# Channel attention on one Trainium2 core: one read of 24 rows issued as two, by partitions

## The chip, the cores and the metric

The kernel runs on one core of one Trainium2 chip. The metric is the device time of one execution in microseconds (us), lower is better. The core's engines are TensorE (PE), VectorE (DVE), ScalarE (ACT), GpSimd (POOL) and SyncE (SP). Data moves between the device memory and the on-chip memory of 128 partitions through 16 DMA engines, which this document calls lanes; here SP issues all reads and ACT issues all writes.

## What is computed

The input x is a picture of 384 x 384 positions with 384 channels in bf16. Per channel a mean and a maximum over all positions are taken; both go through the same two small matrices, and the sigmoid of their sum scales each channel of x:

```python
xf = x.reshape(B, H * W, C)
gap = jnp.mean(xf, 1)
gmp = jnp.amax(xf, 1)
h_a = relu(gap @ w1)
h_m = relu(gmp @ w1)
scale = sigmoid(h_a @ w2 + h_m @ w2)
return x * scale[:, None, None, :]
```

(`relu` and `sigmoid` stand here for the reference's own few lines.) The scale needs all of x, and the product needs all of x again, so the work has two passes over 113.25 MB.

## The kernel before, in words

The 147,456 positions are 1,152 rows of 128 partitions, a row being 384 channels or 768 bytes in each partition. The **first pass** reads all of them in 53 transfers that SP issues in a loop over `steps`, at one line (L371 in the listing). A transfer of m rows puts m x 768 bytes into each of the 128 partitions. For each transfer, PE adds its rows up (`sums`, L274, and `tail_sums`, L290, for the last four transfers), and DVE takes the running maximum into `acc` (`maximum`, L340). For seven groups of 32 rows, the `packed_block`, PE and ACT also squeeze the four parts of eight rows into three (`test`, `pack`; L301, L302, L322, L328, L329), so that they stay on the chip and are not read again; the parts of group i start at row `FIRST_AT[i]` (24 rows) and `FOURTH_AT[i]` (8 rows). Groups 1 to 3 are read in one transfer of 32 rows, the others in one of 24 and one of 8 (group 0's 24 in two pieces).

When the last read of the first pass has landed and DVE has folded `acc` to one row (L346 and L423 turn it over on PE), the small products run and ACT writes the sigmoid, `scale_bc`, at L431. The **second pass** multiplies rows by `scale_bc` on DVE (`multiply`, L436), writes them out from ACT's queue, and reads back what had not stayed on the chip (L529), each new read into the place that a write has left. Packed groups are opened again between these (`unpack`, L468, L473, L487).

The order is written out by hand: the loop over `steps` fixes the order of each engine's instructions. A read waits on SP until its place is free. That is mostly told by DVE, PE or ACT, which have read the rows that stood there. There are also eight landing semaphores, used in turn, so a transfer may have to wait for the one eight places ahead of it. Whoever reads `rows` waits for the landing of the transfer that brought them.

The read that the change touches is the nineteenth of the first pass, the 24 rows of packed group 4 (`FIRST_AT[4]` is 200). It is a transfer of 128 partitions with 18,432 bytes each, 2304 KB. It is followed on SP by the 8 rows of the same group (768 KB) and by the reads of the blocks behind it.

Of the kernel before, what the change touches and what calls it, by code (L numbers as in the profile page):

```python
# [39 lines left out]
FIRST_AT = (0, 104, 40, 64, 200, 176, 152)  # L40
# [12 lines left out]

FIRST_LOAD = 4
FOLD_BEFORE = 2

BETWEEN = (
    ((21, 30), (208, 48)), ((51, 21), (0, 49), (72, 21)), ((208, 51), (0, 46), (46, 34)),
# [29 lines left out]
def kernel(  # L88
# [7 lines left out]
    nc = tc.nc  # L96
    P = nc.NUM_PARTITIONS
# [9 lines left out]
    xr = x.rearrange("b h w c -> (b h w) c")  # L107
    orr = out.rearrange("b h w c -> (b h w) c")

    def rows_of(ap, block):  # L110
        first, n = block
        return ap[first * P:(first + n) * P, :].rearrange("(p n) c -> p n c", n=n)
# [7 lines left out]
    def take(n):  # L120
        nonlocal at
        at += n
        return at - n, n
# [3 lines left out]
    packed_block = take(GP * PACKED)  # L127
# [36 lines left out]
    rows = nc.alloc_sbuf_tensor_at("rows", [P, HELD_ROWS + BODY_ROWS, C], BF16, offset=RING_BYTES).ap()  # L164
# [68 lines left out]
    for i in range(PACKED):  # L233
        if i in TOGETHER:
            lo = min(HOME_AT[i], D_AT[i % 2])
# [34 lines left out]
    def sums(rows, n, done, total):  # L270
        for k in range(0, n, MM_ROWS):
            g = min(MM_ROWS, n - k)
            for q in range(CQ):
                nc.tensor.matmul(  # L274
                    sum_ps[q * QP:q * QP + 1, 0:g * P],
                    lhsT=ones_bf[:, 0:1],
                    rhs=rows[:, k:k + g, q * P:(q + 1) * P],
                    start=(done + k == 0),
                    stop=(done + k + g == total),
                )  # L280

    def turn_sums():
        for r in range(MM_ROWS):
            nc.scalar.copy(out=s_sb[r % 2], in_=sum_ps[:, r * P:(r + 1) * P])  # L284
            nc.tensor.matmul(gsum_ps, lhsT=s_sb[r % 2], rhs=pick, start=(r == 0), stop=False)

    def tail_sums(rows, n, last):
        for k in range(n):
            for q in range(CQ):
                nc.tensor.matmul(  # L290
                    gsum_ps[:, q:q + 1], lhsT=rows[:, k, q * P:(q + 1) * P], rhs=ones_bf,
                    start=False, stop=(last and k == n - 1 and q == CQ - 1),
                )
# [12 lines left out]
    def test(i, what):  # L306

        if what == 2:
            test_one(high(part(i, 3), I8), 5 * i + 4)
            return  # L310
        n = G * C // 2
        a_b = homes[i][:, 0:2 * G, :].rearrange("p (r n) c -> p r (n c)", r=2).bitcast(I8)
        test_one(a_b[:, :, 2 * n * what + 1:2 * n * (what + 1):2], 5 * i + 2 * what)
        test_one(high(part(i, 2), I8)[:, n * what:n * (what + 1)], 5 * i + 2 * what + 1)

    def pack(i, half):
        n = G * C // 2
        span = slice(half * n, (half + 1) * n)
        for c in range(0, n, BANK):
            for r in range(4):  # L320
                for k, dt in enumerate((E4, E3)):
                    nc.tensor.matmul(  # L322
                        words[:, c:c + BANK], lhsT=weights[2 * r + k],
                        rhs=high(part(i, r), dt)[:, half * n + c:half * n + c + BANK],
                        start=(r == 0 and k == 0), stop=(r == 3 and k == 1),
                    )
        for r in (0, 1):
            nc.scalar.copy(out=high(part(i, r), U8)[:, span], in_=low(part(i, r + 2), U8)[:, span])  # L328
        nc.scalar.activation(  # L329
            out=part(i, 2).rearrange("p n c -> p (n c)").bitcast(U16)[:, span], in_=words,  # L330
            func=ACT.Copy, bias=32767.5,
        )

    def judge():
        nc.scalar.activation(out=test_copy, in_=tests[:, 0:NT], func=ACT.Copy, accum_out=test_sum)
        nc.scalar.copy(out=total, in_=test_sum)
        nc.tensor.matmul(bad_ps, lhsT=total, rhs=ones_bf, start=True, stop=True)

    def maximum(out_, in0, in1):
        nc.vector.tensor_tensor(out=out_, in0=in0, in1=in1, op=ALU.max)  # L340

    def turn_over(out_, rows):

        for r in range(LATE_ROWS):
            for q in range(CQ):
                nc.tensor.transpose(  # L346
                    out=out_[:, r, q * P:(q + 1) * P], in_=rows[:, r, q * P:(q + 1) * P], identity=ident_bf
                )
# [3 lines left out]
    def fold():  # L352

        n = folds[-1]
        h = n // 2
        maximum(acc[:, 0:h, :], acc[:, 0:h, :], acc[:, n - h:n, :])
        folds.append(n - h)

    done = turn = nth = 0
    for st in steps:  # L360
        if st[0] == "test":
            test(*st[1:])
        elif st[0] == "pack":
            pack(*st[1:])
        elif st[0] == "judge":
            judge()
        if st[0] != "load":
            continue
        _, block, rows, lo, hi = st
        m = hi - lo  # L370
        nc.sync.dma_start(out=rows, in_=rows_of(xr, block)[:, lo:hi, :])  # L371
        if nth < len(loads) - SUM_TAIL:
            sums(rows, m, done, TOT - tail_rows)
        else:
            tail_sums(rows, m, nth == len(loads) - 1)
        if nth == len(loads) - FOLD_BEFORE:
            fold()
        halves = HALVES if len(folds) == 1 else ((0, folds[-1]),)
        j = max(0, min(m, A - done))
        if j:  # L380
            nc.vector.tensor_copy(out=acc[:, done:done + j, :], in_=rows[:, 0:j, :])
        done += m
        if nth == len(loads) - SUM_TAIL - 1:
            turn_sums()
        while j < m:
            c, e = halves[turn % len(halves)]
            turn += 1
            e = min(e, c + m - j)
            maximum(acc[:, c:e, :], acc[:, c:e, :], rows[:, j:j + e - c, :])
            j += e - c  # L390
        if block == late_block:
            turn_over(late, rows)
        elif block == first_block:
            nc.vector.tensor_copy(out=kept_ps.bitcast(U32), in_=rows[:, 0:PSUM_ROWS, :].bitcast(U32))
            nc.vector.tensor_copy(out=kept_b.bitcast(U32), in_=rows[:, PSUM_ROWS:for_psum, :].bitcast(U32))
        nth += 1
# [164 lines left out]
    for turn in range(turns):  # L561
        b, buf = order.pop(0)
# [56 lines left out]
```

## Time and profile before

| what | value |
|---|---|
| time, median of 3 runs | 725.32 us (725.16 to 725.88) |
| the profiled execution, its own time | 725.41 us |
| its span, first to last instruction | 723.6 us |
| bytes read / written | 192.14 MB / 113.25 MB |
| DMA packets | 20403 |
| DVE busy | 564.1 us (78% of the span) |
| ACT busy | 349.8 us (48%) |
| PE busy | 184.7 us (26%) |

The profile is that of one execution. Its page divides the span into 40 equal slices of 18.09 us and gives, for each, the busy share of each engine and of the DMA lanes and the bytes moved per second. Other views give who waited for whom, the chain of work that ended last, the instructions in order of time, and busy time by stretch. For every transfer the trace also keeps sixteen landing marks, one for each lane that has finished its share, and a record of every packet with its start, length and size.

### The profile page before, as it was taken

The page shows a single profiled execution, that of the slowest core. Times are in us where ns is not written, and L with a number is a line of the kernel's source. Part 1 is how long each engine was busy: PE and PEld are TensorE (multiplying, and loading weights), DVE is VectorE, ACT ScalarE, POOL GpSimd, SP SyncE. Part 2 cuts the span into 40 slices and gives each one's busy share as a digit, 9 for nine tenths or more (in the row PEclk, how much of TensorE's full clock was granted, in tenths as well). Part 3 has the DMA queues.
Part 4 walks back from the last instruction along what each step waited for, and adds up shares of the span by engine and source line. Part 5 has one row for each costly group of instructions (what it writes and reads, how often), then busy time and mean ns, then how long its engine had stood idle before and what let it go on. Part 6 is the DMA issues. An engine that isn't in the chain of part 4 may idle for free.

```text
span 723.6 us, 3882 instructions
## 1 busy us (share of the span) xinstructions
PE 184.7 (26%) x1363; PEld 74.2 (10%) x1363; DVE 564.1 (78%) x445; ACT 349.8 (48%) x251; POOL 0.7 (0%) x6
## 2 busy tenths in 40 slices
PE   5577475965867470000000000000000000001000
PEld 1222122322322140000000000000000000001000
DVE  5699899999999998797966554897888889495200
ACT  6999999997999200056230023806154442200000
POOL 0000000000000000000000000000000000000000
PEclk9888878896988555555555555555555555555555
DMA  9999999999999979999999999999999999999997
GB/s 380 434 438 435 417 442 427 429 430 432 431 426 428 426 312 356 400 433 431 433 431 431 434 428 431 434 430 435 430 429 432 437 432 430 430 433 439 442 426 339
DMA packets 20403, 305.63 MB, mean 422 GB/s; under 512 B 2624, under 2 KB 2976, under 8 KB 7200
## 3 DMA queue, kind: packets, MB, share of 16 engines
q1 hardware_dynamic: 13040, 192.14, 62.3%
q10 hardware_dynamic: 7344, 113.25, 36.6%
q8 instruction: 10, 0.16, 0.1%
q14 instruction: 9, 0.07, 0.0%
HBM read 192.14 MB, written 113.25 MB: 422 GB/s over the span
## 4 chain that ended last, share of the span: by engine, by line
DMA 63%; DVE 25%; issue 3%; PE 2%; ACT 1%; SPq 0%; DVEq 0%; ACTq 0%
DMA rows<-in_x_dram 40%; DMA out_dram<-rows 23%; DVE acc L340 16%; DVE rows L436 9%; PE words_ps L322 1%; ACT rows L328 0%; DVE acc L436 0%; SPq L371 0%; PE bank_a L274 0%; ACT rows L329 0%; ACT rows L487 0%; PE bank_a L430 0%; ACT scale_bc L431 0%; DVE small L424 0%; PE bank_a L423 0%
## 5 line engine op out<-in xcount | busy, mean ns | idle before, releaser
L436 DVE TENSOR_TENSOR rows<-rows,scale_bc 128x9216 bf16<-128x9216 bf16 (+9 forms) x56 | 230.9, 4164 | 91.2 <-DMA rows<-in_x_dram 90.0
L340 DVE TENSOR_TENSOR acc<-acc,rows 128x2304 bf16<-128x2304 bf16 (+4 forms) x227 | 245.0, 1154 | 13.9 <-DMA rows<-in_x_dram 13.6
L487 ACT COPY rows<-rows 128x1536 uint8<-128x1536 uint8 x28 | 41.3, 1476 | 204.2 <-DVE rows L436 144.8
L274 PE MATMUL bank_a<-rows,small 128*1 128x512 bf16 (+3 forms) x897 | 93.3, 466 | 80.9 <-DMA rows<-in_x_dram 76.1
L346 PE MATMUL words_ps<-ident_bf,acc 128*128 128x128 bf16 x24 | 2.7, 310 | 376.3 <-DVE acc L574 376.3
L301 ACT ACTIVATE rows<-rows 128x3072 uint8<-128x3072 int8 (+1 forms) x35 | 81.9, 2341 | 9.1 <-DMA rows<-in_x_dram 8.4
L302 ACT ACTIVATE rows<-rows 128x3072 uint8<-128x3072 uint8 (+1 forms) x35 | 82.0, 2344 | 1.1
L487 ACT COPY rows<-acc 128x1536 uint8<-128x1536 uint8 x42 | 60.5, 1473 | 18.2 <-DVE acc L473 17.7
L274 PEld LDWEIGHTS <-small 128*1 128x1 bf16 x897 | 30.6, 95 | 140.3 <-issue 118.2
L346 PEld LDWEIGHTS <-acc 128*128 128x128 bf16 x24 | 2.5, 144 | 376.7 <-DVE acc L574 376.7
L322 PE MATMUL words_ps<-rows,scale_bc 128*128 128x512 fp8e4 (+1 forms) x126 | 37.9, 414 | 9.2 <-ACT rows L329 9.2
L328 ACT COPY rows<-rows 128x1536 uint8<-128x1536 uint8 x28 | 39.7, 1468 | 0.4 <-PE words_ps L322 0.4
L322 PE MATMUL words_ps<-rows 128*128 128x512 fp8e3 (+1 forms) x126 | 35.8, 394 | 0.0
L468 DVE TENSOR_SCALAR rows<-rows 128x1536 uint16<-128x1536 uint16 x56 | 31.3, 560 | 1.9
L322 PE MATMUL words_ps<-rows,w_sb 128*128 128x512 fp8e3 x84 | 27.0, 405 | 0.0
L487 ACT COPY acc<-rows 128x1536 uint8<-128x1536 uint8 x14 | 20.5, 1466 | 0.0
L329 ACT ACTIVATE rows<-words_ps 128x1536 uint16<-128x1536 f32 x14 | 20.1, 1439 | 0.0
L322 PEld LDWEIGHTS <-scale_bc 128*128 128x128 bf16 x126 | 12.2, 103 | 30.2 <-issue 19.3
L322 PEld LDWEIGHTS <-rows 128*128 128x128 bf16 x126 | 12.9, 102 | 16.7 <-issue 3.3
L473 DVE SCALAR_TENSOR_TENSOR acc<-acc,rows 128x768 uint32<-128x768 uint32 x14 | 13.4, 959 | 0.5
L473 DVE SCALAR_TENSOR_TENSOR rows<-rows 128x768 uint32<-128x768 uint32 x14 | 13.4, 958 | 0.5
L284 ACT COPY w_sb<-bank_a 65x128 f32<-65x128 f32 x2 | 0.5, 261 | 24.5 <-PE bank_a L274 24.0
(61 smaller groups left out, 72.0 us busy)
## 6 DMA issues: line engine op xcount, KB each, us to landing
rows<-in_x_dram SPq DMA_DIRECT2D x16, 2880.0 KB, 25.4
out_dram<-rows ACTq DMA_DIRECT2D x15, 2880.0 KB, 22.8
rows<-in_x_dram SPq DMA_DIRECT2D x15, 2304.0 KB, 20.0
out_dram<-rows ACTq DMA_DIRECT2D x14, 2304.0 KB, 21.1
rows<-in_x_dram SPq DMA_DIRECT2D x4, 3072.0 KB, 31.8
out_dram<-rows ACTq DMA_DIRECT2D x2, 4608.0 KB, 46.7
rows<-in_x_dram SPq DMA_DIRECT2D x9, 768.0 KB, 16.7
rows<-in_x_dram SPq DMA_DIRECT2D x2, 3264.0 KB, 26.4
```

Source lines behind the costliest of these rows:

```text
L274: nc.tensor.matmul(sum_ps[q * QP:q * QP + 1, 0:g * P], lhsT=ones_bf[:, 0:1], rhs=rows[:, k:k + g, q * P:(q + 1) * P], start=(done + k == 0 ...
L301: nc.scalar.activation(out=out_, in_=rows, func=ACT.Square, bias=test_bias, scale=TEST_SCALE)
L302: nc.scalar.activation(out=out_, in_=out_, func=ACT.Square, bias=minus4, accum_out=tests[:, k:k + 1],)
L322: nc.tensor.matmul(words[:, c:c + BANK], lhsT=weights[2 * r + k], rhs=high(part(i, r), dt)[:, half * n + c:half * n + c + BANK], start=(r ...
L328: nc.scalar.copy(out=high(part(i, r), U8)[:, span], in_=low(part(i, r + 2), U8)[:, span])
L329: nc.scalar.activation(out=part(i, 2).rearrange("p n c -> p (n c)").bitcast(U16)[:, span], in_=words, func=ACT.Copy, bias=32767.5,)
L340: nc.vector.tensor_tensor(out=out_, in0=in0, in1=in1, op=ALU.max)
L346: nc.tensor.transpose(out=out_[:, r, q * P:(q + 1) * P], in_=rows[:, r, q * P:(q + 1) * P], identity=ident_bf)
L436: nc.vector.tensor_tensor(out=dst, in0=src, in1=scale_bc.unsqueeze(1).to_broadcast([P, n, C]), op=ALU.mult)
L468: nc.vector.tensor_scalar(out=u16(dst), in0=u16(src), scalar1=s1, scalar2=s2, op0=op0, op1=op1)
L473: nc.vector.scalar_tensor_tensor(out=u32(v), in0=u32(v), scalar=0x3F3F3F3F, in1=u32(m), op0=ALU.bitwise_xor, op1=ALU.bitwise_xor)
L487: nc.scalar.copy(out=dst, in_=src)
```

## The change

The read of the 24 rows of packed group 4 is issued as two: one of partitions 0 to 119 and one of partitions 120 to 127, the same rows and bytes in both together. Nothing else differs; line numbers below L371 move by six.

```diff
 FIRST_LOAD = 4
 FOLD_BEFORE = 2
+
+UNEVEN, FIRST_PARTITIONS = 4, 120
...
         _, block, rows, lo, hi = st
         m = hi - lo
-        nc.sync.dma_start(out=rows, in_=rows_of(xr, block)[:, lo:hi, :])
+        parts = (0, P)
+        if block == packed_block and lo == FIRST_AT[UNEVEN]:
+            parts = (0, FIRST_PARTITIONS, P)
+        for a, b in zip(parts, parts[1:]):
+            nc.sync.dma_start(out=rows[a:b], in_=rows_of(xr, block)[a:b, lo:hi, :])
```

The order of instructions on PE, DVE, ACT and POOL is the same; SP has one more transfer to issue.

## The prediction

> **What bounds the kernel now.** I first read the slices of the page: the DMA share and the bytes moved.
>
> ```profile
> DMA  9999999999999979999999999999999999999997
> GB/s 380 434 438 435 417 442 427 429 430 432 431 426 428 426 312 356 400 433 431 433 431 431 434 428 431 434 430 435 430 429 432 437 432 430 430 433 439 442 426 339
> ```
>
> The lanes are busy from end to end but for the fifteenth and sixteenth slice, which hold the turn between the passes. The rate is the same 430 GB/s whether the lanes read, write or do both: 430 / 16 = 26.9 GB/s a lane. Then the busy time by stretch of the first pass, with columns PE, PEld, DVE, ACT, POOL (busy us and count), granted clock, DMA share and GB/s:
>
> ```profile
> 120.00:140.00 20.00, 12.88 (x99) 4.90 (x101) 18.89 (x18) 19.42 (x13) 0.00 (x0) 0.83 1.00 426
> 140.00:160.00 20.00, 15.78 (x117) 6.41 (x110) 20.00 (x20) 19.81 (x14) 0.00 (x0) 1.00 1.01 433
> 240.00:260.00 20.00, 10.76 (x76) 3.14 (x76) 19.13 (x20) 0.19 (x1) 0.00 (x0) 0.50 1.01 425
> 260.00:280.00 20.00, 10.83 (x126) 7.82 (x125) 17.75 (x22) 1.78 (x7) 0.00 (x0) 0.50 0.73 267
> ```
>
> The DMA share is 1.0 until the pass ends, and DVE is nearly as full. Which of the two ends it is told by DVE's instructions in order of time (start, length, count; in brackets the idle time before):
>
> ```profile
> 184.84 42.44 DVE L340 TENSOR_TENSOR acc<-acc,rows 128x1920 bf16<-128x1920 bf16 x40 [1.13 <-DMA rows<-in_x_dram]
> 227.57 13.11 DVE L340 TENSOR_TENSOR acc<-acc,rows 128x1920 bf16<-128x1920 bf16 x12 [0.29 <-DMA rows<-in_x_dram]
> 241.56 26.48 DVE L340 TENSOR_TENSOR acc<-acc,rows 128x1920 bf16<-128x1920 bf16 x26 [0.87 <-DMA rows<-in_x_dram]
> ```
>
> DVE waits for a landing at 184.8, 227.6 and 241.6 us and never again; from 241.56 on it runs through to the end of the pass. So a landing that comes later at 185 us has 0.29 + 0.87 = 1.2 us of later waits to be lost in, and one at 241.5 us nothing. The chain that ended last says the same for the whole:
>
> ```profile
> DMA 63%; DVE 25%; issue 3%; PE 2%; ACT 1%; SPq 0%; DVEq 0%; ACTq 0%
> ```
>
> I therefore ask one thing of the change: what it does to the slowest lane of the first pass. The second pass starts when the scale is there (L431 at 275.68 us) and has nothing that would absorb a shift, so what the first pass gains or loses goes to the end one for one.
>
> **What the lanes do.** The landing marks show that each lane goes its own way. The read before the changed one has its sixteen marks from 131.8 to 133.5 us, the changed read from 137.3 to 139.0, the last read of the pass from 265.3 to 268.3, with the second slowest at 267.2. A lane that has fallen behind stays behind: a lane always has work queued, and its rate never rises above 26.9 GB/s. In the changed read each lane moves 8 packets of 18,432 bytes, each 0.686 us long and the next one 4 ns before its end: 8 x 0.682 = 5.46 us.
>
> **The change, part by part.**
>
> *SP.* One more issue. The 53 issues at L371 take 0.33 us in the middle, and the changed read is issued at 109.4 us for a landing at 139.0, so SP has 20 us and more in hand: nothing. The landing semaphores rotate by one; "eight places back" stays eight places back and counts the small read as a place. The transfers near it wait for ones that landed 20 us earlier: nothing.
>
> *Waits.* DVE, PE and ACT wait for two landings where they waited for one. An instruction that only waits costs DVE some 0.02 to 0.06 us here: under 0.1 us, and only where DVE isn't behind. Behind such a wait stand the maxima of all later reads, in order.
>
> *How many lanes.* Every large transfer of this kernel has 128 partitions, 8 packets a lane. The only other count is the 96 partitions of w2, whose sixteen lanes have 6 packets each. Equal shares are thus all that the trace shows; 120 can be shared equally by 15 lanes of 8 and 8 by 8 lanes of 1. I take these. Then one lane moves nothing (-5.46 us), seven move what they did, and eight move a ninth packet (+0.68 us). [...]
>
> *Which partitions.* This is the disputed cost. [...] From below: if the rate is the lane's own, the price is that of the ninth packet, 0 to 0.68 us. From above: if four lanes at a time met on one way, each packet would take four times 0.682 and the read 16.4 us longer. I take the smallest sharing that there can be, two lanes on one way, because the one pairing that has been shown at full rate is given up; it is also nearest to the packets that the trace shows at their longest, 1.18 us in place of 0.686 where a lane was disturbed. Then:
> - the 120 partitions: two lanes at half rate, 8 packets in 10.92 us: +5.46;
> - the 8 partitions: if two lanes always halve a way, a block of eight spans two ways and eight lanes meet on them, four on each: a packet of 0.682 takes 2.73;
> - together 5.46 + 2.73 = 8.2 us for the worst lane. Less 0.7, as lanes of a pair don't start together (the marks before lie 1.7 us apart, 0.7 between two lanes on average); less 0.7, as the four don't arrive together; less 0.7, because the slowest lane at the end is 1.1 us behind the next and need not be among those that pay most. That leaves 6.1.
>
> Bounds of this case: 8.2 above; below 5.46 - 1.1 = 4.4, where the slowest lane is one that hardly pays. [...]
>
> **The sum.** The profiled execution took 725.41 us (span 723.6 and 1.8 around it), 0.1 above the median of 725.32. 725.4 + 6.1 = **731.5 us**; with the bounds 729.8 to 733.6.
>
> **The rivals.**
> - *The rate is the lane's own.* No sharing; only the ninth packet counts. If the slowest lane is one of the eight (8 in 16), the landing at 241.5 us comes 0.68 later and so does the end: 726.1. If it is one of the seven, the second slowest, 1.3 us ahead there, doesn't overtake it: 725.4. For it: reads and writes run at exactly the same 26.9 GB/s, and the short packets of w2, on other shares than 8, show no stretching (36 ns as in the 768-byte reads of `acc`), though that transfer is too small to fill a way. Not slower by over 0.2%. It decides as long as fewer than about 1.15 lanes share a way (5.46 x 0.15 and the ninth packet make 1.5 us). 0.18.
> - *The idle lane is the slowest one.* As before, but 1 in 16: DVE's wait before 241.56 shrinks from 0.87 to about 0.2: 724.7. Within 0.2% too, since nothing that DVE waits for after 185 us sums to more than 1.2. 0.02, with 0.02 more for a gain over 0.2% by a way I don't see.
> - *The split isn't what I take it for*: each lane keeps its own partitions in both parts, and only a closing mark is added: 725.4. 0.03.
> - *Four lanes on one way*: 725.4 + 16.4 = 741.8. 0.03.
>
> **Chances and range.** Two on one way: 0.72. A measurement of this kernel can tell about 0.2% (1.45 us) from no change. Slower by over 0.2%: 0.72 + 0.03 = 0.75; within: 0.18 + 0.03 + 0.02 = 0.23; faster: 0.02. The likeliest case alone spans 729.8 to 733.6. To leave out no more than two in ten, the range must reach to the first rival: 725.3 to 733.0.
>
> **What would show it.** Right: a landing of the 2160 KB part some 35 us after its issue where the whole read took 29.6, and its packets at 1.2 to 1.4 us instead of 0.686; the ninth packet longer still; about 6 us x 430 GB/s missing from the slices around 145 us while the DMA share stays at 9; DVE waiting some 5 us more for `rows` between 139 and 185 us; L431 at about 281.8; a second pass like before. Wrong: packets of 0.686 us throughout, which is the first rival, with one lane 5.5 us ahead of the others; or a share of packets other than 8 per lane on 15 lanes. If L431 moves and the end doesn't, the second pass has slack that I deny.

## The result and the profile after

The changed kernel takes **733.51 us** (733.27 to 733.61, 4 runs) where the kernel before took 725.54 beside it: 8.0 us more, ratio 1.011 (95% interval 1.0092 to 1.0127). The prediction was 731.5 with the range 725.3 to 733.0. Its direction holds, and so do packets of twice their length and the path to the end; the three reductions in its sum don't. The cost is 1.3 times the forecast, and the time lies 0.5 us above the range.

The first thing to read is the packet count of the page, here of the kernel before and of the changed one:

```profile
DMA packets 20403, 305.63 MB, mean 422 GB/s; under 512 B 2624, under 2 KB 2976, under 8 KB 7200
DMA packets 20410, 305.63 MB, mean 418 GB/s; under 512 B 2631, under 2 KB 2983, under 8 KB 7207
```

There are 7 more, and the 7 are all among the smallest. The data packets are the same 128, one for each partition; the rest are closing marks of 4 bytes, 16 for each of the 89 transfers of SP before (1,424 records), and 1,431 now. For this read that is 16 before, 16 + 7 = 23 now, one for each lane if 15 lanes and 8 lanes took part. The landing marks say so too: the 120 partitions have fifteen marks between 142.7 and 146.8 us, the 8 partitions eight between 144.3 and 148.4, and each of the two has one further mark early, 0.6 and 0.45 us after its issue. So 15 and 8 lanes took part, as forecast.

Then the slices, which answer to those of before:

```profile
DMA  9999999999999997999999999999999999999997
GB/s 386 425 438 427 434 438 431 251 429 424 438 426 423 423 404 267 393 432 432 434 431 429 435 432 426 435 423 436 429 437 427 437 428 436 431 433 446 417 447 336
```

In the eighth slice, 128 to 146 us, 251 GB/s are left of 430, while the lanes are as busy as ever. The low slice of the turn between the passes has moved from the fifteenth to the sixteenth. Finer, in stretches of 6 us of the changed kernel (columns as before: PE, PEld, DVE, ACT, POOL, clock, DMA share, GB/s):

```profile
126.00:132.00 6.00, 5.61 (x42) 1.99 (x42) 5.56 (x5) 5.90 (x5) 0.00 (x0) 0.65 0.99 415
132.00:138.00 6.00, 5.83 (x44) 2.38 (x41) 5.77 (x7) 5.67 (x5) 0.00 (x0) 1.00 1.07 220
138.00:144.00 6.00, 0.22 (x5) 0.00 (x0) 5.28 (x5) 1.09 (x1) 0.00 (x0) 0.71 0.97 196
144.00:150.00 6.00, 1.56 (x12) 0.50 (x15) 1.48 (x2) 1.52 (x1) 0.00 (x0) 0.50 1.01 350
```

The second and third of these stretches in the kernel before:

```profile
132.00:138.00 6.00, 6.00 (x45) 2.49 (x43) 6.00 (x7) 5.58 (x5) 0.00 (x0) 1.00 0.99 418
138.00:144.00 6.00, 4.76 (x39) 1.82 (x36) 6.00 (x6) 5.97 (x3) 0.00 (x0) 1.00 1.05 451
```

For twelve microseconds the lanes move half of what they can, with a busy share of 1.0: the lanes are at work, and most packets take twice their time. The packet records agree: of the 128 packets of 18,432 bytes of this read, all but one took 0.686 us before, and in the changed kernel they took 1.40 us in the median; 24 took over 1.5 us, the longest 1.97.

Who waits for it is told by DVE's instructions in order of time, first one line of the kernel before, then the changed one:

```profile
126.31 57.40 DVE L340 TENSOR_TENSOR acc<-acc,rows 128x1920 bf16<-128x1920 bf16 x54 [1.11 <-DMA rows<-in_x_dram]
```

```profile
136.38 6.90 DVE L342 TENSOR_TENSOR acc<-acc,rows 128x2304 bf16<-128x2304 bf16 x6 [0.23 <-DMA rows<-in_x_dram]
148.52 6.97 DVE L342 TENSOR_TENSOR acc<-acc,rows 128x2304 bf16<-128x2304 bf16 x7 [5.24 <-DMA rows<-in_x_dram]
157.77 7.37 DVE L342 TENSOR_TENSOR acc<-acc,rows 128x1920 bf16<-128x1920 bf16 x7 [2.27 <-DMA rows<-in_x_dram]
165.92 26.81 DVE L342 TENSOR_TENSOR acc<-acc,rows 128x2304 bf16<-128x2304 bf16 x25 [0.78 <-DMA rows<-in_x_dram]
193.62 82.13 DVE L342 TENSOR_TENSOR acc<-acc,rows 128x1920 bf16<-128x1920 bf16 x78 [0.89 <-DMA rows<-in_x_dram]
```

DVE, which before had no wait for `rows` from 126.3 to 183.7 us, now waits 5.2, 2.3 and 0.8 in that time, and 0.9 at 193.6. The waits at 227.6 and 241.6 us are gone: once DVE has been set back, the later landings are ahead of it. The last read of the pass lands at 276.0 us instead of 268.3, and the scale follows, here before and after:

```profile
275.68 0.49 ACT L431 ACTIVATE scale_bc<-bank_a 128x384 bf16<-128x384 f32 x1 [4.17 <-PE bank_a L430]
283.40 0.49 ACT L437 ACTIVATE scale_bc<-bank_a 128x384 bf16<-128x384 f32 x1 [4.26 <-PE bank_a L436]
```

The chain that ended last, of the whole run, has more of the lanes in it and less of DVE:

```profile
DMA 67%; DVE 23%; issue 2%; PE 1%; SPq 0%; ACT 0%; DVEq 0%; ACTq 0%
```

Of the span's growth of 8.1 us (731.7 against 723.6), 7.7 have come about by the time of the scale; the second pass does the same work 0.4 us slower, with DVE waiting 91.8 us for `rows` instead of 90.0.

### The profile page after: what moved, and what is told of

Its sections match the earlier page's. It is cut to its first block, busy times and chain, and to the rows that moved or that the text cites. A ratio compares the mean times of both kernels' runs of the same rounds, so it can differ in the third digit from the quotient of the medians.

```text
span 731.7 us, 3883 instructions
## 1 busy us (share of the span) xinstructions
PE 186.1 (25%) x1363; PEld 74.4 (10%) x1363; DVE 564.4 (77%) x445; ACT 349.9 (48%) x251; POOL 0.7 (0%) x6
## 4 chain that ended last, share of the span: by engine, by line
DMA 67%; DVE 23%; issue 2%; PE 1%; SPq 0%; ACT 0%; DVEq 0%; ACTq 0%
DMA rows<-in_x_dram 47%; DMA out_dram<-rows 20%; DVE acc L342 14%; DVE rows L442 8%; PE bank_a L276 1%; PE words_ps L324 1%; DVE acc L442 0%; SPq L377 0%; DVE rows L474 0%; PE bank_a L436 0%; ACT scale_bc L437 0%; DVE acc L474 0%; DVE small L430 0%; SPq L535 0%; PE bank_a L429 0%
## 5 line engine op out<-in xcount | busy, mean ns | idle before, releaser
L442 DVE TENSOR_TENSOR rows<-rows,scale_bc 128x9216 bf16<-128x9216 bf16 (+9 forms) x56 | 230.9, 4164 | 92.9 <-DMA rows<-in_x_dram 91.8
L276 PE MATMUL bank_a<-rows,small 128*1 128x512 bf16 (+3 forms) x897 | 95.8, 477 | 88.1 <-DMA rows<-in_x_dram 83.4
L303 ACT ACTIVATE rows<-rows 128x3072 uint8<-128x3072 int8 (+1 forms) x35 | 81.9, 2341 | 17.8 <-DMA rows<-in_x_dram 17.2
```

What stands on the lines that cost most here:

```text
L276: nc.tensor.matmul(sum_ps[q * QP:q * QP + 1, 0:g * P], lhsT=ones_bf[:, 0:1], rhs=rows[:, k:k + g, q * P:(q + 1) * P], start=(done + k == 0 ...
L303: nc.scalar.activation(out=out_, in_=rows, func=ACT.Square, bias=test_bias, scale=TEST_SCALE)
L442: nc.vector.tensor_tensor(out=dst, in0=src, in1=scale_bc.unsqueeze(1).to_broadcast([P, n, C]), op=ALU.mult)
```

## The experiments

All times are medians; "more" is against the kernel before run beside it on the same chip.

### Two transfers, cut by rows

```diff
-        nc.sync.dma_start(out=rows, in_=rows_of(xr, block)[:, lo:hi, :])
+        cuts = (0, m)
+        if block == packed_block and lo == FIRST_AT[4]:
+            cuts = (0, 16, m)
+        for a, b in zip(cuts, cuts[1:]):
+            nc.sync.dma_start(out=rows[:, a:b, :], in_=rows_of(xr, block)[:, lo + a:lo + b, :])
```

> The same read cut in two by rows (16 and 8 rows, all 128 partitions in both). Sharing of ways into the partitions: no lane meets another one, so no change, 725.5 us within 0.3. Rival, the second transfer with its landing and waits is what costs: the 8 us come back, 733.5.

Measured 725.59 us against 725.76, ratio 0.9999 (0.9989 to 1.0009). A second transfer, its landing and its waits cost nothing that these runs can tell. What costs is the cut by partitions.

### Cut in halves, 64 and 64 partitions

```diff
-UNEVEN, FIRST_PARTITIONS = 4, 120
+UNEVEN, FIRST_PARTITIONS = 4, 64
```

> The same read cut at partition 64, 64 and 64. Sharing of ways: 64 partitions reach half of the ways, so two lanes stand on each in both halves; every lane has 8 packets at half rate, 5.46 us more and no ninth packet: 730.5 to 731.0 us. Rival, uneven shares (an idle lane, a ninth packet) are what costs: 16 lanes can have 4 packets each in either half, no change, 725.5. Rival, the rate is the lane's own: 725.5.

Measured 732.31 against 725.76, 6.6 us more, ratio 1.0104 (1.0082 to 1.0127). Its packet count is 20419, 16 more than before, so sixteen lanes take part in each half, and no lane idles. Still, the packets of this read take 1.385 us in the median instead of 0.686, and the rate halves, as the stretches of this kernel show:

```profile
132.00:138.00 6.00, 4.92 (x37) 2.09 (x38) 5.43 (x7) 6.00 (x5) 0.00 (x0) 1.00 1.03 227
138.00:144.00 6.00, 0.43 (x6) 0.00 (x0) 5.49 (x5) 0.77 (x1) 0.00 (x0) 0.88 0.96 210
```

Neither uneven shares nor a rate of the lane's own survive this. The lanes run at half their rate, 210 to 227 GB/s of 430, as if two at a time stood on one way; that 64 partitions reach half of the ways was an assumption of mine, and no run shows a way by itself. The cost lies above the bare 5.46, and the interval (6.0 to 9.2 us) leaves that out.

Nor does any run show by itself whether what the lanes share lies on the side of the partitions or of the device memory: in every cut the places in x move with the partitions. The 48-row halves below speak for the partitions. They are read from one unbroken stretch of x, while the pieces of this read, one for each partition, lie 224 rows of 768 bytes apart in it, and in both the packets double (2.89 us for 1.364 there, 1.385 for 0.686 here).

### The small read alone, early and late

The read of group 4 stays whole. Partitions 120 to 127 of the same 24 rows are read once more, earlier, into the same place; 0.147 MB are thus read twice.

```diff
+        if block == packed_block and lo == FOURTH_AT[2]:
+            g = slice(120, 128)
+            nc.sync.dma_start(
+                out=homes[4][g], in_=rows_of(xr, packed_block)[g, FIRST_AT[4]:FIRST_AT[4] + 3 * G, :]
+            )
         nc.sync.dma_start(out=rows, in_=rows_of(xr, block)[:, lo:hi, :])
```

> The read of group 4 stays whole; 24 rows of partitions 120 to 127 are read once more, earlier (ahead of group 2), into the same place: the small read alone, as an addition of 0.147 MB. Sharing of ways: eight lanes with one packet each on two ways, 2.73 us if all eight arrive together, less as they don't: 727.0 to 728.2 us. Rival, no sharing: eight lanes carry one packet more, 0 to 0.7 us, 725.5 to 726.2.

Measured 728.00 against 725.76, 2.2 more, ratio 1.0035 (1.0021 to 1.0049). Then the same ahead of the first block (`if block == first_block`):

> The extra read of partitions 120 to 127 (24 rows, 0.147 MB more) moved to the fourth place of the first pass, ahead of the first block. Sharing of ways: as in its later place, where it cost 2.2 us: 727.5 to 728.4. Rival, that cost came from its place (the lanes lay 2 us apart there, here under 1 us): 726.3 or less.

Measured 728.04 against 725.90, 2.1 more, 1.0032 (1.0020 to 1.0044). Eight packets of 0.68 us, one to a lane, cost three times one of them, at both places of the pass. In the second run they took 1.07 to 2.40 us each.

### Eight partitions four apart

The same extra read with `g = slice(0, 32, 4)`: eight partitions four apart, with the same bytes. That eight lanes would then meet on no way, and cost one packet at the most, was my estimate.

> [...] Sharing of ways: 0 to 0.7 us, 725.5 to 726.2. Rival, a transfer of 8 partitions is slow in itself: the same as with partitions 120 to 127, 727.0 to 728.2.

Measured 736.80, 11.0 more, ratio 1.0164 (1.0145 to 1.0183). Neither expectation meets it, and for another reason: SP issued this read at 69.7 us and not at 29.5, as it had to wait for ACT first, and everything behind it on SP with it. The lanes ran dry, which the page of this run shows in its fourth slice:

```profile
GB/s 384 426 437 159 438 422 433 430 438 426 433 429 426 428 423 271 398 427 429 433 432 434 433 432 428 432 429 432 431 438 425 439 425 439 424 439 439 431 436 346
```

The read of partitions 120 to 127 at this place has no such wait; the two differ in their partitions alone. A second try, ahead of the first block:

> [...] At this place SP should wait only a few us for ACT, while the lanes still have three reads queued, which the 70 us wait of the first try spoilt. Sharing of ways: 0 to 0.7 us, 725.5 to 726.4. Rival, a transfer of 8 partitions is slow in itself: as with partitions 120 to 127 at this place.

Measured 755.74, 29.8 more, ratio 1.0408 (1.0391 to 1.0425): SP waited to 36.9 us here. As times both are lost. But the read went out to idle lanes, and its packets can be looked at by themselves: 1.27 us from the first start to the last end. For the neighbour to compare, the extra read of partitions 120 to 127 was made the first transfer of the kernel (`if nth == 0`):

> The extra read of partitions 120 to 127 as the very first transfer, on idle lanes. In the run where SP's wait let the lanes run dry, eight packets to partitions 0, 4 to 28 took 1.26 us from the first start to the last end. Sharing of ways: four lanes on each of two ways, 2.7 us or more from first start to last end. Rival, a transfer of 8 partitions is the same wherever they lie: 1.3 us.

Here the eight packets run from 1.69 to 3.90 us, 2.2 from the first start to the last end, and the last landing mark stands at 5.5 us, 3.8 after the first start; with partitions four apart it was at 40.0, 1.6 after. Eight packets of the same size thus took 2.2 us to partitions side by side and 1.27 us to partitions four apart. The 2.2 us fall short of the 2.7 that were expected, other reads came up behind both, and one of the two is the kernel's first transfer, so it tells the direction and not the factor. The one run of this kernel took 727.39 us.

### The 120 partitions alone

The changed kernel, with its small read moved to the fourth place of the pass.

```diff
+        if block == first_block:
+            g = slice(120, 128)
+            nc.sync.dma_start(
+                out=homes[4][g], in_=rows_of(xr, packed_block)[g, FIRST_AT[4]:FIRST_AT[4] + 3 * G, :]
+            )
+        own = slice(0, 120) if block == packed_block and lo == FIRST_AT[4] else slice(0, P)
-        nc.sync.dma_start(out=rows, in_=rows_of(xr, block)[:, lo:hi, :])
+        nc.sync.dma_start(out=rows[own], in_=rows_of(xr, block)[own, lo:hi, :])
```

> The changed kernel with its small read (partitions 120 to 127) moved to the fourth place of the first pass, the 120 partitions staying where they are. The reductions for lanes that don't start together hold: 5.46 - 1.4 and 2.2 for the small read make 731.8 or less. Rival, the lanes' offsets save nothing, because lanes that are ahead take from the ways of those behind: the half-and-half cut cost 6.6 for the same 8 packets, so 6.6 + 2.2 make 734.4.

Measured 735.44 against 725.90, 9.5 more, ratio 1.0129 (1.0112 to 1.0146), which is also 1.0 above the rival's 734.4. The run with the extra read at the same place took 728.04, so if the two costs simply add, the 120 partitions instead of 128 cost 735.44 - 728.04 = 7.4 us by themselves; the two intervals put together leave some 1.5 either way. The lanes also lay further apart ahead of the cut here, 2.3 us instead of 1.7. Two lanes at half rate make 5.46. My reductions are the wrong way round here: the offsets of the lanes don't save, something comes on top.

### A third of the bytes, at two places

The changed kernel's cut on the 8-row read of group 4 instead of its 24-row read.

```diff
-        if block == packed_block and lo == FIRST_AT[UNEVEN]:
+        if block == packed_block and lo == FOURTH_AT[UNEVEN]:
```

> The 120 and 8 cut on the 8-row read of group 4 in place of its 24-row read: a third of the bytes. A reduction of 2.1 us that belongs to the lanes' offsets and not to the size: 8.2 / 3 - 2.1 = 0.6, 726.2. Rival, no reduction, the cost goes with the bytes: 8.0 / 3 = 2.7, 728.3.

Measured 729.51 against 725.90, 3.6 more, 1.0048 (1.0032 to 1.0065). Both expectations lie below it. From 8 to 24 rows the cost goes from 3.6 to 8.0: taken at face value, 0.28 a row and 1.4 that doesn't go with the rows, on top. Then the cut on the 8-row read of group 0 (`lo == FOURTH_AT[0]`), where the lanes lie closer:

> The 120 and 8 cut on the 8-row read of group 0, the third of the pass, where the lanes lie 0.8 us apart (1.9 us at the read of group 4, where the same cut cost 3.6). If the lanes' offsets are what adds to the bare 2.7: 2.7 to 3.0, 728.6 to 728.9. If the addition is there without offsets, from lanes that are through early and stand in the ways of the others: 3.5, 729.4. My first arithmetic, offsets save: 728.6 or less.

Measured 728.08 against 725.92, 2.2 more, 1.0030 (1.0018 to 1.0041). Less than where the lanes lay further apart (1.7 us by the landing marks, not the 1.9 that the expectation says), and less than the bare 2.7: of the three expectations, only that of my first arithmetic, in which offsets save, meets it. In microseconds the intervals are 2.3 to 4.7 and 1.3 to 3.0, and both take in 2.7, so the pair points to the offsets but doesn't settle it. The next pair has more bytes.

### Halves of 48 rows, early

```diff
-UNEVEN, FIRST_PARTITIONS = 4, 120
+UNEVEN, FIRST_PARTITIONS = 4, 64
...
-        if block == packed_block and lo == FIRST_AT[UNEVEN]:
+        if block == between[0][1]:
```

> The half-and-half cut on the 48-row read of the sixth place, where the lanes lie 0.8 us apart: twice the bytes of the cut on the 24-row read of group 4 (lanes 1.7 us apart), which cost 6.6 where two lanes at half rate make 5.46. If what comes on top is from lanes that lie apart, being ahead of or behind each other: close to the bare 2 x 5.46 = 10.9, 736.5 to 737.3. Rival, it belongs to the sharing itself and goes with the bytes: 2 x 6.6 = 13.2, 739.1.

Measured 737.78 against 726.13, 11.7 more, ratio 1.0156 (1.0142 to 1.0170), that is 10.3 to 12.3 us. It takes in the bare 10.9 and leaves out 13.2. What comes on top of two lanes at half rate doesn't go with the bytes in full; it is 0.7 here and 1.1 in the cut on 24 rows further on, a difference that the intervals can't tell from none. Some of it lies in the packets alone: those of this read took 2.89 us in the median where they took 1.364 before, 2.1 times as long and not twice. And the read before it was hardly set back, with its marks 0.9 us apart, where those of the read before the halves of group 4 lay 4.9 apart.

### Two cuts

The 120 and 8 cut on the 24-row reads of groups 4 and 5.

```diff
-        if block == packed_block and lo == FIRST_AT[UNEVEN]:
+        if block == packed_block and lo in (FIRST_AT[UNEVEN], FIRST_AT[UNEVEN + 1]):
```

> The 120 and 8 cut on the 24-row reads of groups 4 and 5. Cost by bytes through shared ways: twice 8.0, 741.5 to 742. Rival, one cut's cost is in part what the lanes lose by lying apart, which the first has already made (4 us and one lane 5.5 ahead): 739 or less.

Measured 742.30 against 725.92, 16.4 more, 1.0225 (1.0206 to 1.0245): twice 8.2. As far as the interval tells (15.0 to 17.8 us), the second cut costs what the first did, though its lanes start further apart.

## Why the prediction was right in kind and short in size

- **What bounds the pass.** Right. The lanes are its limit, DVE follows with nothing in hand, and the turn moved by 7.7 us, the end by 8.0. The signs that it named came, each larger: the 120 partitions landed 37.4 us after their issue instead of 35, and the scale was written at 283.40 instead of 281.8. One small reading was off, and nothing rests on it: at 241.5 us the second slowest lane was 1.2 us ahead, not 1.3.
- **SP and the waits at nothing.** Right: the cut by rows has the same second transfer and the same added waits and costs nothing that can be told.
- **Equal shares on 15 and 8 lanes.** Right in the number of lanes, by the closing marks. In the read of 8 rows behind the cut, one mark stands at 135.97, ten us ahead of the other fifteen, as that of a lane with no part in either read would. The records name neither the lane nor the partition of a packet, so which lane meets which partitions isn't seen in any trace, nor that the pairing of the uncut read is given up, as the choice of two lanes on one way assumed.
- **Two lanes on one way.** Right in what it forecast, against the first rival: packets of 1.40 us instead of 0.686 with the DMA share at 1.0, and halves of 64 and 64 that cost 6.6 us with sixteen lanes at work. The ninth packet and the idle lane, which that rival counted with, play no part in that run. The rival with the idle lane as the slowest fell with it. Four lanes on one way, by the estimate from 0.682 us a packet, would have made packets of 2.7 us and 741.8 in all. The two terms of the sum, 5.46 for two lanes on one way and 2.73 for a block of eight that spans two ways, are estimates: no run shows the ways that they speak of. In their place the runs showed 6.6 us for the halves, 7.4 for the 120 partitions as the difference of two runs, and 2.2 and 2.1 for the small read.
- **The small read.** About right: 2.73 less 0.7 makes 2.0, measured 2.2 and 2.1 by itself.
- **The 120 partitions less 0.7, and less another 0.7 for the slowest lane at the end.** This is the term that failed. I had 5.46 - 1.4 = 4.1; by the difference of two runs it is 7.4. I took lanes that don't start together to miss each other, and the slowest lane to be one that may pay little. The marks of the 8 rows read behind the cut show that no lane pays little but the idle one: they lay from 139.15 to 140.85 us, and fifteen of them now lie from 146.48 to 149.96, so that each of these lanes lost at least 5.6. Compared in their order, fourteen marks lie 7.3 to 8.2 later and the last 9.1; at the end of the pass they all lie 7.4 to 8.6 later, the last one 7.6.
- **Lanes out of step.** That they miss each other isn't what the trace shows; the last packets of a whole read got longer once the cut one had begun. The read *before* the changed one shows it: its landing marks lay from 131.8 to 133.5 us, and lie from 131.7 to 136.3 now. Lanes through with it began on the 120 partitions from 131.3 on, and of the last packets of the old read some took up to 2.08 us instead of 0.912, more than two lanes at half rate each would make of it (1.82). In their order, the ten early marks haven't moved and the six late ones have. How much of the 7.4 this makes isn't shown, as behind the cut the marks in the middle have moved nearly as far as the last.
- **The sum.** Apart, the two parts cost 9.5 us, together 8.0. That is close to the bare sum without any reduction, 5.46 + 2.73 = 8.2, and two cuts took 16.4, twice that. What the forecast of 6.1 lacks are thus 1.9 of the 2.1 that the three reductions took off. Of these, the small read's holds by itself, and the two of the 120 partitions don't. That the bare sum fits so well is luck in part: the 120 partitions cost more than 5.46, and the two reads together less than apart. Together, the small read adds some 0.6 to the 7.4; why so little isn't shown.
- **The range.** The likeliest case's own bounds were 729.8 to 733.6, and they hold the time. I cut the range at 733.0 to make room for the rival below. It should have kept the whole upper part of the case that had 0.72.

What stays open: how the 1.9 us on top of 5.46 in the 120 partitions divide between lanes that lie apart, packets that take a little over twice their time, and the odd count of lanes (fifteen can't all be in pairs). The 48-row halves show that the part on top doesn't go with the bytes in full, and the two 8-row cuts point to the offsets; two cuts in a row, which cost twice the one, don't. Eight partitions four apart couldn't be timed within the pass, because of SP's wait.

## What to carry to other kernels

In this kernel, where the lanes were the limit, a transfer of 128 partitions was worth keeping whole: the cut by the rows cost nothing that could be told (725.59 against 725.76 us), the cuts of the same read by the partitions 8.0 and 6.6 us. They left the busy share of the lanes at 1.0 and halved the rate (220 and 196 GB/s where the kernel before had 418 and 451), so read the GB/s beside the share, and the length of a packet beside both. And being out of step wasn't a saving to count on: by the estimate of two lanes at half rate each, the cuts here cost between 0.6 us less than that and 1.9 more, and the last packets of the read ahead of the cut took up to 2.08 us instead of 0.912.

## What the runs showed of the hardware that I had not expected

The cut read slowed whole ones beside it: packets of the 128-partition read before it took up to 2.08 us instead of 0.912, and those of the read behind it 0.40 us in the median instead of 0.234. And 24 of the 128 packets of the changed read took over 1.5 us, where two lanes at half rate each make 1.37. Even in the 48-row halves, with the lanes close together, packets of 36,864 bytes took 2.1 times as long as before (2.89 us instead of 1.364), a little over the twice that two lanes at half rate each make.
